# Loading the last head's output-projection rows once: 28 heads on 112 partitions, three heads in rows of 3 KB

## The chip, the cores and the metric

The kernel runs on one core of one Trainium2 chip. The time is the device time in microseconds (us) of one execution; a time given for a kernel is the median of several executions. Beside these, one execution was taken by the hardware profiler, which gives the start and length of every instruction and DMA packet. The engines are called PE (TensorE: matmuls, with its weight loads listed apart as PEld), DVE (VectorE), ACT (ScalarE), POOL (GpSimd) and SP (SyncE, which here issues nearly all DMA transfers). Memory on the chip has 128 partitions.

## The reference, cut to what matters

One token is decoded by an attention block and, beside it, by a SwiGLU block; a sigmoid gate mixes the two. All data are bf16.

```
x = A_x                                              # [1, 1, 512]
g = sigmoid((x * gate_w).sum(-1))
q = (x @ wq) as 32 heads of 128
p = softmax(q . k_cache^T * 128**-0.5)               # k_cache, v_cache: [1, 32, 65536, 128]
o = p @ v_cache                                      # 32 heads of 128, side by side: 4096 values
a = o @ wo                                           # wo: [4096, 512]
b = (silu(x @ w_gate) * (x @ w_up)) @ w_down         # w_gate, w_up: [512, 1792]; w_down: [1792, 512]
out = g * a + (1 - g) * b
```

The two caches hold 1074 MB of the 1088 MB that the kernel reads; every byte of a cache is used once.

## The kernel before, in words

**Tiling.** A head's K or V is two transfers of 8 MB (64 KB on each of 128 partitions, A and B half) into `ring`, a buffer of 176 KB per partition whose parts are used over and over. DVE turns the K rows in chunks into `kt` (four buffers, line 277), PE makes scores from a turned chunk (line 345) into `psS`; the softmax runs over POOL (195, 198), ACT (232) and DVE (301); PE then multiplies 256 + 256 weight tiles of V with the probabilities (line 352) into `psO`. DVE scales a head's output into `lt` (line 291), while the next head is already under way.

**Queues.** SP's program (lines 131 to 177) is an order written out by hand, with semaphore waits that hold a transfer until its place in `ring` is free. For each head it has: K's A half, the head before's V B half, K's B half, V's A half. All of it goes to one DMA queue, which works in order. A semaphore rises by 16 when a transfer has landed.

**The start.** The query projection weights `wq` are loaded first, then head 0's K in four pieces. PE projects the query (line 333), ACT copies it (216), PE spreads it with the constant `sel` (339), ACT copies it to `qd` and `zq` (220, 210), and then scores can begin. POOL builds `sel` and the identity `ident` in lines 181 to 190: two memsets and five affine selects, the last of which raises `s_sel`, on which PE waits in line 337.

**The output projection of heads 0 to 30.** It is done in the last head (number L = 31), in PE's block `pe_wo` (line 417), between the B half of head 30's V and the B half of head 31's scores. `wo` lies in the first 32 KB of `ring`, with 32 consecutive rows of `wo` on each partition: partitions 0 to 123 hold heads 0 to 30, and partitions 124 to 127 hold the rows of head 31, which meet zeros. It comes as two transfers of 16 KB on each of 128 partitions (lines 156 to 159), each after a wait for DVE to have turned the K that lay there. PE spreads the head outputs `lt` with `ident` to the same layout (line 420, into `psW`), ACT copies that to `om` (226), and PE multiplies column j of `om` with row j of every partition in `rows` (lines 358 and 359, half of the 512 outputs each). The last of these raises `s_wod`, after which SP issues the SwiGLU weights into the same place (164 to 166).

**The last head's rows.** Line 167 loads rows 3968 to 4095 of `wo`, 1 KB on each of 128 partitions, once more as `wo1`, since head 31's output comes at the very end. PE waits for them in line 431 (`s_wo1`), in its last block `pe_end`, and uses them in line 435 with `o31`, between the last two 128-row pieces of the down weights.

**The SwiGLU and the end.** PE's block `pe_mlp` (402 to 415) makes gate and up (line 408) and multiplies 12 of the 14 pieces of the down weights (414, after waits for `s_gu` and `s_wd`). After it PE multiplies the B half of head 31's V, which comes in six pieces (`PARTS`, line 113), the last ones small. Then come the last two down-weight pieces (`s_wd2`, `s_wd3`), two copies, and the output's transfer.

**Buffers at the start.** `xrow` and `gwrow` (1 KB per partition) and `xg` (2 KB) serve only the gate's sum at the start (lines 126, 212, 263, 324).

Of the kernel before, what the change touches and what calls it, by code (L numbers as in the profile page):

```python
# [5 lines left out]
P = 128  # L6
KB = 1024
# [8 lines left out]
ALU = mybir.AluOpType  # L16
ACT = mybir.ActivationFunctionType
ET = mybir.EngineType
BF16 = mybir.dt.bfloat16
F32 = mybir.dt.float32  # L20
# [6 lines left out]
def bass_gated_mix__mha_block_cached__swiglu_ffn__decode_kernel(  # L27
# [13 lines left out]
    _, H, S, Dh = A_k_cache.shape  # L41
    D = A_wq.shape[0]
# [5 lines left out]
    SCALE = float(Dh) ** -0.5  # L48
    assert Dh == 128 and D == 512 and F % P == 0 and ROWS == 256 and H == 32
    L = H - 1  # L50
    A_ORDER = list(range(NCH // 2, NCH)) + list(range(NCH // 2))
    B_ORDER = list(range(NCH))
    PER = 2 * NCH

    with ExitStack() as ctx:
        def sb(name, shape, dt):
            return ctx.enter_context(nc.sbuf_tensor(name, shape, dt))
# [12 lines left out]
        psW = psum("psW", [P, 512], F32)  # L70
# [8 lines left out]
        lt = sb("lt", [P, 4 * (P + 4) + 4], BF16)  # L79
        ident = sb("ident", [P, P], BF16)  # L80
        sel = sb("sel", [P, 4, 128], BF16)
        om = sb("om", [P, 32], BF16)
        o31 = sb("o31", [P, 2], BF16)
        ones1 = sb("ones1", [P, 2], BF16)
        onesr = sb("onesr", [P, P], F32)
        xrow = sb("xrow", [P, D], BF16)
        gwrow = sb("gwrow", [P, D], BF16)
        xg = sb("xg", [P, D], F32)
        fin = sb("fin", [P, D], BF16)
        sc = sb("sc", [P, 8], F32)  # L90
        xTb = sb("xTb", [P, 16], BF16)
# [17 lines left out]
        def at(byte, n):  # L109
            return ring[:, byte // 2:byte // 2 + n]  # L110
# [7 lines left out]
        wu_ap = at(WU, Dc * F).rearrange("p (c m j) -> p c m j", c=Dc, j=FC)  # L118
        wd_ap = at(WD, FC * D).rearrange("p (c n) -> p c n", c=FC)
        wo_ap = at(WO, 32 * D).rearrange("p (j n) -> p j n", j=32)  # L120
        wo1_ap = at(WO1, D)
        ktb = [kt[:, b, :].bitcast(BF16).rearrange("p (j n e) -> p j n e", j=2, e=2) for b in range(NB)]
        zw = [[zq[:, je, 31 - c:31 - c + P] for c in range(2 * NCH)] for je in range(4)]
# [7 lines left out]
        @block.sync  # L131
        def _(sp):
            def load(dst, src, s):
                sp.dma_start(dst, src).then_inc(sm[s], 16)  # L134

            def place(kind, h, u, s):
                byte = {"k": (K_A, K_B), "v": (V_A, V_B)}[kind][u]
                load(at(byte, ROWS * Dh), kv_dram[kind][h, u], s)

            k0 = kv_dram["k"][0, 0]  # L140
            k1 = kv_dram["k"][0, 1]
            half = ROWS * Dh // 2
            load(at(K_A + 2 * half, half), k0[:, half:2 * half], "s_ka")
            load(at(K_A, half), k0[:, 0:half], "s_k0a")
            load(at(K_B + 2 * half, half), k1[:, half:2 * half], "s_k0b")
            sp.wait_ge(sm["ktd"], NCH // 2)
            load(at(K_B, half), k1[:, 0:half], "s_kb")
            sp.wait_ge(sm["s_q"], 1)
            place("v", 0, 0, "s_va")
            for r in range(1, H):  # L150
                sp.wait_ge(sm["ktd"], PER * r - NCH // 2)
                place("k", r, 0, "s_ka")
                sp.wait_ge(sm["va1"], r)
                place("v", r - 1, 1, "s_vb")
                if r == L:
                    wo_dram = A_wo.rearrange("(p j) n -> p (j n)", j=32)
                    for q in range(2):
                        sp.wait_ge(sm["ktd"], PER * r + 3 * NCH // 4 + q * NCH // 4)
                        load(at(WO + q * 16 * KB, 16 * D), wo_dram[:, q * 16 * D:(q + 1) * 16 * D], "s_wo")
                sp.wait_ge(sm["ktd"], PER * r + NCH // 2)  # L160
                place("k", r, 1, "s_kb")
                sp.wait_ge(sm["vbd"], r + 1)
                place("v", r, 0, "s_va")
            sp.wait_ge(sm["s_wod"], 1)
            load(at(WG, Dc * F), B_w_gate.rearrange("(p c) f -> p (c f)", c=Dc), "s_wg")
            load(at(WU, Dc * F), B_w_up.rearrange("(p c) f -> p (c f)", c=Dc), "s_wu")
            load(at(WO1, D), A_wo[L * Dh:H * Dh, :], "s_wo1")
            sp.wait_ge(sm["ktd"], PER * H)
            wd_dram = B_w_down.rearrange("(p c) n -> p (c n)", c=FC)
            load(at(WD, WD_CUT * D), wd_dram[:, 0:WD_CUT * D], "s_wd")  # L170
            last = kv_dram["v"][L, 1]
            for n, ((r0, r1), s) in enumerate(zip(PARTS, MARKS)):
                if n == 1:
                    sp.wait_ge(sm["va1"], H)
                load(at(V_B + r0 * 256, (r1 - r0) * Dh), last[:, r0 * Dh:r1 * Dh], s)
            for j, s in ((FC - 2, "s_wd2"), (FC - 1, "s_wd3")):
                load(at(WD + 2 * j * D, D), wd_dram[:, j * D:(j + 1) * D], s)

        @block.gpsimd
        def _(pool):  # L180
            nc.gpsimd.memset(ident[:], 0.0)
            nc.gpsimd.memset(sel[:], 0.0).then_inc(sm["s_sel0"], 1)  # L182
            pool.wait_ge(sm["s_sel0"], 1)
            for je in range(4):
                off = 64 * (je // 2) + je % 2
                v = sel[:, je, :].rearrange("p (g d) -> p g d", g=4)
                last = nc.gpsimd.affine_select(out=v, in_=v, compare_op=ALU.not_equal, fill=1.0, base=-off,  # L187
                                               pattern=[[0, 4], [-2, 32]], channel_multiplier=1)
            nc.gpsimd.affine_select(out=ident[:], in_=ident[:], compare_op=ALU.not_equal, fill=1.0, base=0,  # L189
                                    pattern=[[-1, P]], channel_multiplier=1).then_inc(sm["s_sel"], 1)  # L190
            for m, n in enumerate(MARKS[1:]):
                nc.gpsimd.memset(hbuf[:, m], 0.0).then_inc(sm[n], 16 * L)  # L192
            for h in range(H):
                pool.wait_ge(sm["s_mx"], h + 1)
                nc.gpsimd.partition_all_reduce(amx, mxs, P, RMAX).then_inc(sm["s_ar"], 1)  # L195
                pool.wait_ge(sm["s_exp"], h + 2)
                pool.wait_ge(sm["s_li"], h + 1)  # L197
                nc.gpsimd.partition_all_reduce(Lt, rsum, P, RADD).then_inc(sm["s_L"], 1)  # L198

        @block.scalar  # L200
        def _(act):
# [21 lines left out]
            for h in range(H):  # L223
                if h == L:
                    act.wait_ge(sm["s_o"], 1)
                    nc.scalar.copy(om[:], psW[:, 0:32]).then_inc(sm["s_om"], 1)
                act.wait_ge(sm["s_ar"], h + 1)
                nc.scalar.mul(nbias, amx, -SCALE).then_inc(sm["s_nb"], 1)  # L228
                act.wait_ge(sm["s_nb"], h + 1)
                if h:  # L230
                    act.wait_ge(sm["s_pb"], h)
                nc.scalar.activation(pa[:], psS[:], ACT.Exp, bias=nbias, scale=SCALE,  # L232
                                     accum_out=rsum).then_inc(sm["s_exp"], 1)
                if h < L:
                    take_q(h + 1)
# [83 lines left out]
        def _(pe):  # L319
# [82 lines left out]
            with nc.body("pe_mlp", valid_engines=only):  # L402
                pe.wait_ge(sm["s_wg"], 16)
                pe.wait_ge(sm["s_wu"], 16)
                for j in range(FC):
                    for w, o in ((wg_ap, 64), (wu_ap, 80)):
                        for c in range(Dc):
                            last = nc.tensor.matmul(psM[:, o + j:o + j + 1], w[:, c, :, j], xTb[:, c:c + 1],  # L408
                                                    start=(c == 0), stop=(c == Dc - 1))
                last.then_inc(sm["s_h"], 1)  # L410
                pe.wait_ge(sm["s_gu"], 1)
                pe.wait_ge(sm["s_wd"], 16)
                for j in range(WD_CUT):
                    rows(guT[:, j:j + 1], wd_ap[:, j, :])
                nc.br("pe_vb", engines=only)

            with nc.body("pe_wo", valid_engines=only):
                pe.wait_ge(sm["s_otn"], H + 1)
                for q in range(4):
                    last = nc.tensor.matmul(psW[:, 0:32], lt[:, 4 + (P + 4) * q:4 + (P + 4) * q + P],  # L420
                                            ident[:, 32 * q:32 * q + 32], start=(q == 0), stop=(q == 3))
                last.then_inc(sm["s_o"], 1)
                pe.wait_ge(sm["s_om"], 1)
                pe.wait_ge(sm["s_wo"], 32)
                for j in range(32):
                    last = rows(om[:, j:j + 1], wo_ap[:, j, :], first=(j == 0))
                last[1].then_inc(sm["s_wod"], 1)
                nc.br("pe_kb", engines=only)

            nc.switch_bb("pe_end")  # L430
            pe.wait_ge(sm["s_wo1"], 16)
            pe.wait_ge(sm["s_wd2"], 16)
            rows(guT[:, FC - 2:FC - 1], wd_ap[:, FC - 2, :])
            pe.wait_ge(sm["s_o31"], 1)
# [36 lines left out]
```

## Time and profile before

| what | value |
|---|---|
| time, median of 3 runs (lowest to highest) | 2519.21 us (2519.11 to 2519.81) |
| the profiled execution's own time | 2519.56 us |
| its span, from the first to the last instruction | 2518.1 us |
| instructions | 45868 |
| read from HBM | 1087.77 MB, 432 GB/s over the span |
| busy: PE, PEld, DVE | 62%, 33%, 49% |
| busy: ACT, POOL | 2%, 1% |
| mean granted TensorE clock | 0.725 of full speed |

Times inside the trace are counted from the start of the span. A line of instructions has the start, the length, the engine, the kernel's line, the operation, what it writes and reads, and in brackets how long the engine had idled and what ended that. SPq is SP issuing a transfer: its length is that of issuing, not of the data's coming. In a line of waits the numbers are the total in us, how often, and the longest. A DMA packet is one contiguous piece that one of the core's 16 DMA engines moves, or the 4-byte write to a semaphore behind a transfer.

### The profile page before, as it was taken

Reading aid. Unit: us, or ns where it says so; the run is one execution under the profiler, and the core shown is the slowest. Engines: PE = TensorE matmul, PEld = TensorE weight load, DVE = VectorE, ACT = ScalarE, POOL = GpSimd, SP = SyncE. Lnnn points to the kernel's source line nnn. Section 1 sums busy time; section 2 is a strip of 40 time slices with the busy share of each in tenths; the row PEclk is TensorE's granted clock in tenths of the full one; section 3 lists DMA queues with packets and bytes.
Section 4 is the critical chain, followed back from the end, with each engine's and each line's share of the span. In section 5 each row is a group of like instructions: output and inputs, shape, how many; then the busy total and the mean of one; then the engine's idle time right before and its main releaser. Section 6 shows DMA issues by size and latency. Waiting matters only on the chain.

```text
span 2518.1 us, 45868 instructions
## 1 busy us (share of the span) xinstructions
PE 1561.7 (62%) x20700; PEld 837.3 (33%) x20828; DVE 1221.5 (49%) x1176; ACT 40.3 (2%) x138; POOL 26.1 (1%) x80
## 2 busy tenths in 40 slices
PE   4665755756657556566575575665755656656666
PEld 2333323323333233332332332333323333333234
DVE  4453553544535536445355354453553544545533
ACT  0000000000000000000000000000000000000000
POOL 0000000000000000000000000000000000000000
PEclk9776776767767677677677776776777767767776
DMA  9999999999999999999999999999999999999999
GB/s 417 435 435 433 433 435 434 433 433 433 433 433 433 433 433 433 433 433 433 433 433 433 433 433 434 434 433 435 436 433 433 433 434 433 433 433 433 434 432 393
DMA packets 20755, 1087.94 MB, mean 432 GB/s; under 512 B 2308, under 2 KB 2951, under 8 KB 3079
## 3 DMA queue, kind: packets, MB, share of 16 engines
q1 hardware_dynamic: 20736, 1087.78, 99.9%
q8 instruction: 8, 0.13, 0.0%
q14 instruction: 5, 0.03, 0.0%
q10 hardware_dynamic: 6, 0.00, 0.0%
HBM read 1087.77 MB, written 0.00 MB: 432 GB/s over the span
## 4 chain that ended last, share of the span: by engine, by line
issue 96%; ACT 1%; POOL 1%; DMA 1%; PE 0%; SPq 0%; DVE 0%; POOLq 0%
ACT pa L232 1%; DMA ring<-in_B_w_down_dram 1%; POOL st L198 0%; POOL st L195 0%; ACT st L228 0%; PE psO L352 0%; SPq L134 0%; POOL sel L187 0%; PE psY L358 0%; DVE pb L301 0%; POOLq L197 0%; POOL sel L182 0%; DVE fin L316 0%; POOL hbuf L192 0%; POOL ident L189 0%
## 5 line engine op out<-in xcount | busy, mean ns | idle before, releaser
L345 PE MATMUL psS<-kt,zq 128*128 128x512 bf16 x3968 | 1104.3, 424 | 827.9 <-DVE kt L277 805.4
L277 DVE STREAM_TRANSPOSE kt<-ring 128x1024 uint32<-128x1024 uint32 x1024 | 1163.2, 1206 | 925.2 <-DMA ring<-in_A_k_cache_dram 925.2
L345 PEld LDWEIGHTS psS<-kt,zq 128*128 128x128 bf16 x4096 | 387.4, 105 | 1518.1 <-DVE kt L277 1054.0
L352 PE MATMUL psO<-pb,ring 128*128 128x1 bf16 x16384 | 439.1, 164 | 109.7 <-DVE pb L301 102.5
L352 PEld LDWEIGHTS psO<-pb,ring 128*128 128x128 bf16 x16384 | 433.6, 101 | 140.7 <-issue 122.2
L291 DVE TENSOR_SCALAR lt<-psO,st,sc 128x4 f32 x32 | 9.4, 293 | 247.2 <-PE psO L352 247.2
L301 DVE STREAM_TRANSPOSE pb<-pa 128x512 bf16<-128x512 bf16 x32 | 22.8, 711 | 48.8 <-ACT pa L232 48.8
L228 ACT ACTIVATE st<-st 128x1 f32<-128x1 f32 x32 | 6.5, 203 | 2384.2 <-POOL st L195 2384.2
L299 DVE TENSOR_REDUCE st<-psS 128x1 f32<-128x512 f32 x32 | 22.1, 691 | 37.4 <-PE psS L345 37.4
L195 POOL PARTITION_ALL_REDUCE st<-st x32 | 11.3, 353 | 2410.1 <-DVE st L299 2410.1
L232 ACT ACTIVATE pa<-psS,st 128x512 bf16<-128x512 f32 x32 | 22.0, 687 | 1.0
L198 POOL PARTITION_ALL_REDUCE st<-st x32 | 12.3, 385 | 36.4 <-ACT pa L232 36.4
L210 ACT COPY zq<-qd 128x16 bf16<-128x16 bf16 x32 | 7.9, 248 | 0.0
L314 DVE TENSOR_TENSOR o<-psO,st 128x1 bf16<-128x1 f32 x1 | 0.2, 161 | 14.6 <-PE psO L352 14.6
L308 DVE TENSOR_SCALAR hbuf<-hbuf 128x14 f32<-128x14 f32 x1 | 0.2, 174 | 13.9 <-ACT hbuf L237 13.9
L408 PE MATMUL psM<-xTb,ring 128*128 128x1 bf16 x112 | 6.9, 198 | 0.0
L408 PEld LDWEIGHTS psM<-xTb,ring 128*128 128x128 bf16 x112 | 6.8, 163 | 0.0
L358 PE MATMUL psY<-ring,om 128*1 128x256 bf16 x32 | 4.9, 327 | 2.3 <-DMA ring<-in_A_wo_dram 2.3
L333 PE MATMUL psM<-xTb,ring 128*128 128x1 bf16 x128 | 3.6, 165 | 4.3 <-DMA ring<-in_A_wq_dram 4.3
L232 ACT ACTIVATION_READ_ACCUMULATOR pa<-psS,st 128x1 f32 x32 | 6.2, 193 | 0.0
L324 PE MATMUL psM<-ones,xrow 1*128 1x1 bf16 x4 | 0.3, 172 | 7.9 <-DMA gwrow<-in_gate_w_dram 7.9
L333 PEld LDWEIGHTS psM<-xTb,ring 128*128 128x128 bf16 x128 | 3.5, 104 | 4.4 <-issue 4.4
(57 smaller groups left out, 39.4 us busy)
## 6 DMA issues: line engine op xcount, KB each, us to landing
ring<-in_A_k_cache_dram SPq DMA_DIRECT2D x4, 4096.0 KB, 27.4
ring<-in_A_wq_dram SPq DMA_DIRECT2D x1, 4096.0 KB, 12.6
ring<-in_A_wo_dram SPq DMA_DIRECT2D x2, 2048.0 KB, 10.6
ring<-in_A_v_cache_dram SPq DMA_DIRECT2D x1, 3776.0 KB, 18.1
ring<-in_A_v_cache_dram SPq DMA_DIRECT2D x1, 2048.0 KB, 18.3
ring<-in_B_w_gate_dram SPq DMA_DIRECT2D x1, 1792.0 KB, 37.9
ring<-in_B_w_up_dram SPq DMA_DIRECT2D x1, 1792.0 KB, 41.9
ring<-in_B_w_down_dram SPq DMA_DIRECT2D x1, 1536.0 KB, 13.8
```

The source lines that it names most:

```text
L195: nc.gpsimd.partition_all_reduce(amx, mxs, P, RMAX).then_inc(sm["s_ar"], 1)
L198: nc.gpsimd.partition_all_reduce(Lt, rsum, P, RADD).then_inc(sm["s_L"], 1)
L210: nc.scalar.copy(zq[:, :, 31:128:32], qd[:, h]).then_inc(sm["s_zq"], 1)
L232: nc.scalar.activation(pa[:], psS[:], ACT.Exp, bias=nbias, scale=SCALE, accum_out=rsum).then_inc(sm["s_exp"], 1)
L277: nc.vector.transpose(o, src).then_inc(sm["ktd"], 1)
L291: nc.vector.tensor_scalar(lt[:, bass.ds(i * 4, 4, P + 5)], psO[:, 0:1].to_broadcast([P, 4]), Li, sc[:, 3:4], ALU.mult, ALU.mult).then_inc( ...
L299: nc.vector.reduce_max(mxs, psS[:], AX_X).then_inc(sm["s_mx"], 1)
L301: nc.vector.transpose(pb[:], pa[:]).then_inc(sm["s_pb"], 1)
L333: last = nc.tensor.matmul(psM[:, 128 + h:129 + h], wq_ap[:, c, h * Dh:(h + 1) * Dh], xTb[:, c:c + 1], start=(c == 0), stop=(c == Dc - 1))
L345: last = nc.tensor.matmul(psS[:], zw[je][c], ktb[n % NB][:, je // 2, :, je % 2], start=first and je == 0, stop=stop and je == 3)
L352: last = nc.tensor.matmul(psO[:, 0:1], at(base + r * 256, Dh), pb[:, col:col + 1], start=first and n == 0, stop=stop and n == len(rows) - 1)
L408: last = nc.tensor.matmul(psM[:, o + j:o + j + 1], w[:, c, :, j], xTb[:, c:c + 1], start=(c == 0), stop=(c == Dc - 1))
```

## The change

Heads 0 to 27 of `wo` (3584 rows) are laid out as before, 32 rows to a partition, but on 112 partitions, still in two transfers of 16 KB per partition. Heads 28 to 30 (384 rows) come in a third transfer, three rows (3 KB) to each of 128 partitions, into a new buffer `xwo` that takes in the former `xrow`, `gwrow` and `xg`. Head 31's rows are loaded by line 167 alone. For the new layout POOL builds a constant `spread` (1152 elements per partition: one memset, one affine select) before `sel`'s affine selects; PE has nine matmuls of one column more ahead of ACT's copy (35 columns instead of 32), multiplies on 112 partitions, and has three further pairs of row products. PE's wait for `s_wo1` stands in `pe_mlp`, ahead of that for `s_wd`, instead of in `pe_end`.

```diff
+    WP = 112
+    HX = WP // 4
+    NX = L - HX
...
+        spread = sb("spread", [P, NX, NX, P], BF16)
+        om = sb("om", [P, 32 + NX], BF16)
...
-        xrow = sb("xrow", [P, D], BF16)
-        gwrow = sb("gwrow", [P, D], BF16)
-        xg = sb("xg", [P, D], F32)
+        xwo = sb("xwo", [P, 4 * D], BF16)
+        xrow, gwrow, xg = xwo[:, 0:D], xwo[:, D:2 * D], xwo[:, 2 * D:4 * D].bitcast(F32)
+        wox = xwo[:, 0:NX * D]
...
+        wox_ap = wox.rearrange("p (j n) -> p j n", j=NX)
...
-                    wo_dram = A_wo.rearrange("(p j) n -> p (j n)", j=32)
+                    wo_dram = A_wo[0:32 * WP, :].rearrange("(p j) n -> p (j n)", j=32)
                     for q in range(2):
                         sp.wait_ge(sm["ktd"], PER * r + 3 * NCH // 4 + q * NCH // 4)
-                        load(at(WO + q * 16 * KB, 16 * D), wo_dram[:, q * 16 * D:(q + 1) * 16 * D], "s_wo")
+                        load(at(WO + q * 16 * KB, 16 * D)[0:WP, :], wo_dram[:, q * 16 * D:(q + 1) * 16 * D], "s_wo")
+                    load(wox, A_wo[32 * WP:L * Dh, :].rearrange("(p j) n -> p (j n)", j=NX), "s_wo")
...
             nc.gpsimd.memset(ident[:], 0.0)
+            nc.gpsimd.memset(spread[:], 0.0)
             nc.gpsimd.memset(sel[:], 0.0).then_inc(sm["s_sel0"], 1)
             pool.wait_ge(sm["s_sel0"], 1)
+            nc.gpsimd.affine_select(out=spread[:], in_=spread[:], compare_op=ALU.not_equal, fill=1.0, base=0,
+                                    pattern=[[P, NX], [-1, NX], [-NX, P]], channel_multiplier=1)
...
-                    nc.scalar.copy(om[:], psW[:, 0:32]).then_inc(sm["s_om"], 1)
+                    nc.scalar.copy(om[:], psW[:, 0:32 + NX]).then_inc(sm["s_om"], 1)
...
                 pe.wait_ge(sm["s_gu"], 1)
+                pe.wait_ge(sm["s_wo1"], 16)
                 pe.wait_ge(sm["s_wd"], 16)
...
                 for q in range(4):
-                    last = nc.tensor.matmul(psW[:, 0:32], lt[:, 4 + (P + 4) * q:4 + (P + 4) * q + P],
-                                            ident[:, 32 * q:32 * q + 32], start=(q == 0), stop=(q == 3))
+                    nc.tensor.matmul(psW[:, 0:32], lt[:, 4 + (P + 4) * q:4 + (P + 4) * q + P],
+                                     ident[:, 32 * q:32 * q + 32], start=(q == 0), stop=(q == 3))
+                for j in range(NX):
+                    for x in range(NX):
+                        c = 4 + 4 * (HX + x)
+                        last = nc.tensor.matmul(psW[:, 32 + j:33 + j], spread[:, x, j, :], lt[:, c:c + 1],
+                                                start=(x == 0), stop=(x == NX - 1))
                 last.then_inc(sm["s_o"], 1)
                 pe.wait_ge(sm["s_om"], 1)
-                pe.wait_ge(sm["s_wo"], 32)
+                pe.wait_ge(sm["s_wo"], 48)
                 for j in range(32):
-                    last = rows(om[:, j:j + 1], wo_ap[:, j, :], first=(j == 0))
+                    rows(om[0:WP, j:j + 1], wo_ap[0:WP, j, :], first=(j == 0))
+                for j in range(NX):
+                    last = rows(om[:, 32 + j:33 + j], wox_ap[:, j, :])
                 last[1].then_inc(sm["s_wod"], 1)
                 nc.br("pe_kb", engines=only)
 
             nc.switch_bb("pe_end")
-            pe.wait_ge(sm["s_wo1"], 16)
             pe.wait_ge(sm["s_wd2"], 16)
```

More of the change, by code (lines that the diff above doesn't have):

```diff
@@ L81, in bass_gated_mix__mha_block_cached__swiglu_ffn__decode_kernel @@
         sel = sb("sel", [P, 4, 128], BF16)
-        om = sb("om", [P, 32], BF16)
+        spread = sb("spread", [P, NX, NX, P], BF16)
+        om = sb("om", [P, 32 + NX], BF16)
         o31 = sb("o31", [P, 2], BF16)
```

## The prediction, made before the changed kernel ran

> **What bounds the kernel now.** I read the page first: its rows by slices, then the DMA queues.
>
> ```profile
> span 2518.1 us, 45868 instructions
> ...
> DMA  9999999999999999999999999999999999999999
> GB/s 417 435 435 433 433 435 434 433 433 433 433 433 433 433 433 433 433 433 433 433 433 433 433 433 434 434 433 435 436 433 433 433 434 433 433 433 433 434 432 393
> ...
> q1 hardware_dynamic: 20736, 1087.78, 99.9%
> ```
>
> SP's queue (q1) holds the 16 DMA engines for 99.9% of the span, at 433 GB/s in nearly every slice, while PE is busy 62% and DVE 49%. The packets confirm it: the queue's first starts at 1.73 us, its last ends at 2515.47 us, and in any 0.5 us between, hardly an exception, 16 of 16 engines have one in hand. So the time is 1.7 us of start, what each engine must move, and a tail; anything else counts only if it lets that queue run dry.
>
> The chain of waits shows the tail (start, length, what):
>
> ```profile
> 2493.62 21.95 DMA ring<-in_B_w_down_dram
> 2515.57 0.14 issue
> 2515.70 0.37 PE psY L358
> ...
> 2516.54 0.41 DVE fin L316
> ```
>
> The last packets are the down weights' last kilobytes; 2.5 us after they land the span ends. Then the two stages that the change touches, in order of time. First the start:
>
> ```profile
> 0.72 0.21 POOL L181 MEMSET ident<- 128x128 bf16 x1 [0.29 <-POOLq L456]
> ...
> 0.86 0.53 POOL L182 MEMSET sel<- 128x512 bf16 x1
> ...
> 13.94 1.10 POOL L187 TENSOR_SCALAR_AFFINE_SELECT sel<-sel 128x128 bf16<-128x128 bf16 x4 [12.54 <-issue]
> 15.00 0.28 POOL L189 TENSOR_SCALAR_AFFINE_SELECT ident<-ident 128x128 bf16<-128x128 bf16 x1
> ...
> 17.32 0.19 PEld L339 LDWEIGHTS psQ<-qTb,sel 128*128 128x128 bf16 x4 [0.36 <-ACT qTb L216]
> ...
> 19.52 0.26 ACT L210 COPY zq<-qd 128x16 bf16<-128x16 bf16 x1
> 24.05 1.25 DVE L277 STREAM_TRANSPOSE kt<-ring 128x1024 uint32<-128x1024 uint32 x1 [14.10 <-DMA ring<-in_A_k_cache_dram]
> ```
>
> POOL's constants are ready at 15.28 us; PE takes them at 17.32; the query is ready at 19.78; scores begin when the first K chunk is turned, at 25.3 us. And the last head:
>
> ```profile
> 2428.93 4.83 SPq L134 DMA_DIRECT2D ring<-in_A_wo_dram  x2
> ...
> 2433.81 0.43 SPq L134 DMA_DIRECT2D ring<-in_A_k_cache_dram  x1
> ...
> 2441.82 0.29 PE L420 MATMUL psW<-ident,lt 128*128 128x32 bf16 x4 [0.50 <-DVE lt L291]
> 2442.14 0.19 ACT L226 CAST om<-psW 128x32 bf16<-128x32 f32 x1 [44.02 <-PE psW L420]
> ...
> 2444.36 0.37 PE L358 MATMUL psY<-ring,om 128*1 128x256 bf16 x1 [2.25 <-DMA ring<-in_A_wo_dram]
> ...
> 2449.31 0.33 SPq L134 DMA_DIRECT2D ring<-in_B_w_gate_dram  x1
> ...
> 2463.69 18.15 DVE L277 STREAM_TRANSPOSE kt<-ring 128x1024 uint32<-128x1024 uint32 x16 [21.92 <-DMA ring<-in_A_k_cache_dram]
> ```
>
> PE has `om` at 2442.33 and waits 2 us for `wo`; its row products end at 2449.27; then PE and DVE idle until K's B half lands at 2463.69.
>
> **The bytes.** The change loads 3968 + 128 rows of 1 KB instead of 4096 + 128: 131072 bytes less, 0.30 us at 433 GB/s. By packets: those of 16 KB took 615 ns (median), of 1792 bytes 74 ns, of 4608 bytes 180 ns, of 1 KB 46 ns, of 64 KB 2422 ns, a semaphore write 9 ns. Between the rows of 1792 and 4608 bytes, one of 3072 takes 74 + 1280/2816 x 106 = 122 ns. Before, each engine moves 2 x 8 packets of 16 KB, 9.84 us. After, if 112 rows share out evenly, 2 x 7 packets (8.61), 8 of 3 KB (0.98) and one semaphore write more (0.01): 9.60 us. That is **-0.24 us**, all on the path, since all engines are full.
>
> How 112 rows share out, no row shows. The queue's 20736 packets are 144 transfers (the sum of the issues on the page) x (128 + 16): 128 rows always go to 16 engines. The three one-row transfers (x, the gate weights, the output) make six packets, one engine each. So the number of engines follows the shape. I bound it: 16 engines with 7 rows each, -0.24 us; 14 engines with 8 rows each, where those 14 keep their 9.84 us and get 0.99 more, +0.99 us; eight engines with 14 rows, 28 x 0.615 + 0.99 - 9.84 = +8.4 us; and one, 224 x 0.615 + 0.99 - 9.84 = +129 us. I take the first: 112 is 16 x 7, and 128, its nearest row, is shared out evenly.
>
> [...]
>
> The third load's memory side is one contiguous block of 128 x 3 KB, the same kind as `wq` (128 x 32 KB), which landed in 12.6 us with 16 engines at work; so it costs as reckoned.
>
> **SP.** One more issue, 0.43 us by the row of its neighbour at 2433.81. Behind it stands K's B half, issued at 2434.3 then. The queue holds both `wo` transfers until 2444.2; 9.9 us of cover, no cost. If the cover were gone it would cost those 0.43 us.
>
> **POOL at the start.** The memset: 0.53 us for 512 elements and 0.21 for 128 give 0.83 ns each, 1.06 us for 1152. The affine select: 0.275 us for 128 elements, nine times that is 2.5 us; between 0.28 (if the time were all fixed) and, as a doubling for its pattern of three dimensions, 5.0. I take 2.5; 3.5 us in all, 6.1 at most. Whether the 12.54 us wait moves with the memset I can't tell; I let it. `s_sel` then comes at 18.8 instead of 15.28, 1.5 us too late for PE; the query is ready at 21.3, still 4 us before the first turned chunk. Cover in all: 2.05 + 5.5 = 7.6 us. No cost. The other way round, constants that come later can't gain anything.
>
> **PE in the last head.** Nine matmuls of one column with their weight loads: 0.25 us at the 28 ns of the query projection (128 in 3.55 us), 1.5 us at that row's single length of 165 ns. `om` comes at 2443.9 at worst; `wo`, all of it, lands some 0.24 us earlier than 2444.3, so cover is left: 0.2 us, thin, and then 14 us before K's B half lands. Three further pairs of products: 0.11 us (2448.67 to 2448.78) to 0.21 us a pair, 0.6 at most. `s_wod` and SP's gate-weight issue come by about 0.4 us later than 2449.31; behind that issue stand the up weights and `wo1`, but the queue holds V's A half until 2482.9 (41.6 us after its issue at 2441.35). No cost. Rows of products on 112 partitions instead of 128: same columns, same time.
>
> **The moved wait.** `wo1` lands 41.8 us after its issue at 2450.16, at 2492.0, and PE reaches the down-weight block at 2501.06, after `guT`. Cover 9.1 us: nothing waits. Behind it would stand 12 down-weight pieces and the 192 V tiles. In `pe_end` the wait goes from ahead of one that ends later anyway; at most the 0.14 us between landing and first matmul, and I take nothing, since the last two kilobytes of down weights still have to land.
>
> **Code.** Some 30 more PE instructions and one more transfer in SP's program. Instruction fetches come as 16 KB packets of their own queue (eight, 0.94 to 1.07 us each); the 64 KB packet beside the one at 2446 us took 3.02 instead of 2.42 us. One more fetch would cost one engine up to 0.6 us. Since engines end 0.5 us apart (last starts 2514.88 to 2515.42), that is +0.1 to +0.6 us at the end; I take no further fetch.
>
> **Sum.** -0.24 us. The profiled execution took 2519.56 us, 1.46 beyond its span, and would take 2519.3; it stands 0.35 above the median of the runs, from which the forecast is 2519.21 - 0.24 = **2519.0 us**. A difference under 0.2% (5 us) is about what can't be told from no change here.
>
> **Rivals.** *A fetch, or a shifted tail, eats the gain*: up to +0.6 - 0.24, 2519.6 us. For it: fetches do fall into this stage (2446 us). Against: the added code is some 30 instructions beside some 1280 matmuls and weight loads of PE's loop, which with the rest took only eight fetches.
> *14 engines*: 2520.2 us. For it: 8 rows per engine is what every transfer here has. Against: nothing forces it when 7 fit.
> *Few engines, slower*: eight engines give 2527.6 us, one 2648; it passes the 5 us mark when the fullest engine gets more than 23 of the 224 row packets, 11 or 12 rows a transfer. For it: one-row transfers use a single engine. Against: 112 has factors of 16 and 14.
> *POOL lets the queue run dry at the start*: needs more than 7.6 us on POOL before scores are late, and then SP's next K piece (issued after 33 us) is late against a queue that is full until 40 us (16.8 MB issued by then at 433 GB/s). Only some 13 us begin to cost and 18 cost 5 us. Against: 6.1 us at most.
>
> **Chances.** As reckoned, 80%; gain eaten, 9%; 14 engines, 7%; few engines 2%; POOL 1%; something unseen on the fast side 1%. Range of the first alone: 2518.6 to 2519.4, as the runs before spread. The whole range reaches to 14 engines: 2518.5 to 2520.3. Slower by over 0.2% are few engines and POOL, 3%; faster 1%; within, 96%.
>
> **What would show it.** SP's queue with 20736 - 32 + 144 = 20848 packets and 1087.65 MB (20844 packets if 14 engines); `zq` copied by 22 us and the first transpose still at about 24 us; PE's wait for `wo` still ended by the DMA; the gate weights issued near 2449.7; no wait on `wo1`; the same 2.5 us tail. Wrong it would be if the DMA row showed a slice under 9, or the last packets of the engines ended over 1 us apart.

## The result, and the profile after

The changed kernel takes 2528.66 us (median of 7 runs, 2527.01 to 2530.29), the kernel before, measured beside it, 2519.69 us (7 runs, 2519.08 to 2519.95). The ratio is 1.0036, 95% interval 1.0026 to 1.0045: slower by 9 us, where 2519.0 us was forecast, in a range up to 2520.3.

The page of the changed kernel, first its span, the rows by slices and the DMA queues:

```profile
span 2527.6 us, 46029 instructions
...
DMA  9999999999999999999999999999999999999999
GB/s 422 432 431 434 432 437 434 431 436 434 431 432 433 437 434 432 434 435 432 432 431 437 435 432 432 435 432 432 432 437 435 432 432 434 434 431 434 437 366 390
...
q1 hardware_dynamic: 20848, 1087.64, 99.9%
...
HBM read 1087.64 MB, written 0.00 MB: 430 GB/s over the span
```

The bytes are those forecast to 0.01 MB (1087.64 against 1087.65), and so are the packets, 20848: the loads of `wo` ran on 16 engines. In the records of packets one packet of an engine starts where its last one ends, so the engines' chains can be followed: in most of them stand 7 packets of 16 KB, a semaphore write, 7 more and another write. The DMA row shows no gap either. But the last slice but one, which holds the loads of `wo`, moved 366 GB/s instead of 432. A DMA engine that is busy need not be moving at its speed: the share of busy time hides this here, and the GB/s shows it.

The same six microseconds of both kernels, in the middle of the `wo` loads. The columns are the stretch, its length, busy time of PE, PEld, DVE, ACT and POOL, the granted clock, the DMA engines' busy share, GB/s. First before, then after:

```profile
2432.00:2438.00 6.00, 5.90 (x147) 4.14 (x146) 1.41 (x2) 0.00 (x0) 0.00 (x0) 0.89 0.93 396
```

```profile
2432.00:2438.00 6.00, 3.74 (x66) 2.04 (x66) 1.29 (x2) 0.00 (x0) 0.00 (x0) 1.00 0.89 208
```

About the same busy share, half the bytes. The DMA issues of the changed kernel say which transfers it is (KB each, median us from issue to landing):

```profile
ring<-in_A_wo_dram SPq DMA_DIRECT2D x2, 1792.0 KB, 16.9
...
xwo<-in_A_wo_dram SPq DMA_DIRECT2D x1, 384.0 KB, 20.2
```

Before, the two larger transfers took 10.6 us:

```profile
ring<-in_A_wo_dram SPq DMA_DIRECT2D x2, 2048.0 KB, 10.6
```

In the trace's records of packets, the 224 packets of 16 KB on 112 partitions took 1157 ns on the mean (659 to 1692), where the 256 on 128 partitions had taken 615 (611 to 625).

The end of the timeline is the old one, some 9.5 us later, with the copy of the output starting 0.9 us after the last landing at 2525.16:

```profile
2525.20 0.37 PE L367 MATMUL psY<-ring,guT 128*1 128x256 bf16 x1
...
2526.04 0.41 DVE L325 CAST fin<-psY 1x256 bf16<-1x256 f32 x1 [0.73 <-PE psY L367]
...
2526.48 0.23 ACTq L250 DMA_DIRECT2D out_dram<-fin  x1
```

**Where the 9.5 us of the profiled executions (2529.07 against 2519.56) are**, per engine, from the packets:

| packets | before | after | difference, us per engine |
|---|---|---|---|
| `wo`, 16 KB | 16 of 615 ns | 14 of 1157 ns | 16.20 - 9.84 = +6.36 |
| third load, 3 KB | none | 8 of 216 ns, reckoned 122 | +1.73 |
| 64 KB packets of V and K just ahead of and behind the `wo` loads | 2422 ns | 26 of them slower, up to 4036 ns, 19.5 us in all | 19.5 / 16 = +1.22 |
| sum | | | +9.31 |

For the rest, 0.2 us, no row was found.

### The profile page after: what moved, and what is told of

Same layout as the page of the kernel before. It is cut to its first block, busy times and chain, and to the rows that moved or that the text cites. A ratio compares the mean times of both kernels' runs of the same rounds, so it can differ in the third digit from the quotient of the medians.

```text
span 2527.6 us, 46029 instructions
## 1 busy us (share of the span) xinstructions
PE 1593.4 (63%) x20843; PEld 838.6 (33%) x20843; DVE 1221.6 (48%) x1176; ACT 40.3 (2%) x138; POOL 28.3 (1%) x82
## 3 DMA queue, kind: packets, MB, share of 16 engines
q1 hardware_dynamic: 20848, 1087.64, 99.9%
HBM read 1087.64 MB, written 0.00 MB: 430 GB/s over the span
## 4 chain that ended last, share of the span: by engine, by line
issue 96%; ACT 1%; POOL 1%; DMA 1%; PE 0%; SPq 0%; DVE 0%; POOLq 0%
ACT pa L241 1%; DMA ring<-in_B_w_down_dram 1%; POOL st L207 0%; POOL st L204 0%; ACT st L237 0%; PE psO L361 0%; SPq L139 0%; POOL spread L191 0%; POOL sel L196 0%; POOL spread L188 0%; PE psY L367 0%; DVE pb L310 0%; POOLq L206 0%; POOL sel L189 0%; DVE fin L325 0%
## 5 line engine op out<-in xcount | busy, mean ns | idle before, releaser
L354 PE MATMUL psS<-kt,zq 128*128 128x512 bf16 x4096 | 1134.2, 426 | 796.7 <-DVE kt L286 778.6
L367 PE MATMUL psY<-ring,om 112*1 112x256 bf16 x32 | 6.2, 384 | 9.6 <-DMA xwo<-in_A_wo_dram 9.6
L368 PE MATMUL psZ<-ring,om 112*1 112x256 bf16 x32 | 6.2, 386 | 0.0
## 6 DMA issues: line engine op xcount, KB each, us to landing
ring<-in_A_wo_dram SPq DMA_DIRECT2D x2, 1792.0 KB, 16.9
```

The costliest lines, as they stand in the source:

```text
L354: last = nc.tensor.matmul(psS[:], zw[je][c], ktb[n % NB][:, je // 2, :, je % 2], start=first and je == 0, stop=stop and je == 3)
L367: a = nc.tensor.matmul(psY[0:1, 0:half], lhs, rhs[:, 0:half], start=first, stop=stop)
```

## The experiments

Each is compared with the kernel before in the same series of runs.

**Is it the transfers over 112 partitions, or the rest of the change?** Two kernels split the change. The first keeps all of it but gives the two big loads 128 partitions again:

```diff
-                    wo_dram = A_wo[0:32 * WP, :].rearrange("(p j) n -> p (j n)", j=32)
+                    wo_dram = A_wo.rearrange("(p j) n -> p (j n)", j=32)
...
-                        load(at(WO + q * 16 * KB, 16 * D)[0:WP, :], wo_dram[:, q * 16 * D:(q + 1) * 16 * D], "s_wo")
+                        load(at(WO + q * 16 * KB, 16 * D), wo_dram[:, q * 16 * D:(q + 1) * 16 * D], "s_wo")
```

> The changed kernel, with its two big wo loads on all 128 partitions again (as before: 32 rows each, head 31's rows among them, unused); the third load of 3 KB rows, spread, the 35 columns and the moved wait stay. Theory 1 (the transfers over 112 partitions are slow in themselves: in the changed kernel's trace their 16 KB packets take 1157 ns on the mean, 615 before): back to packets of 615 ns, 3 KB packets at the reckoned 122 ns, so 2519.7 + 0.98 = 2520.7 us. Theory 2 (the cost lies in the rest: the third load, its wait, PE's and POOL's new work, the longer code): it stays near 2528.7 us.

Measured: 2520.12 us against 2519.58, ratio 1.0003 (0.9993 to 1.0012). The 16 KB packets took 615 ns again, the 3 KB packets 122.6, just as reckoned; the last packet ended at 2516.41 us in the trace against 2515.47 before, the +0.94 that those eight packets cost. So beyond these packets the third load, its wait, `spread`, PE's nine matmuls and the moved wait cost nothing that shows, and the loss goes with the 112 partitions.

The second does that one part alone, in the kernel before:

```diff
-                        load(at(WO + q * 16 * KB, 16 * D), wo_dram[:, q * 16 * D:(q + 1) * 16 * D], "s_wo")
+                        load(at(WO + q * 16 * KB, 16 * D)[0:112, :], wo_dram[0:112, q * 16 * D:(q + 1) * 16 * D], "s_wo")
```

> The kernel before, with nothing changed but that its two wo loads take 112 partitions instead of 128 (the rows of heads 28 to 31 are not loaded, so what PE multiplies with there is old data: the output leaves out three heads). Theory 1: 14 packets of some 1157 ns per engine instead of 16 of 615, +6.4 us, and up to 1 us more from neighbouring packets: 2526 to 2527 us. Theory 2: 14 x 0.615 instead of 16 x 0.615, 2518.5 us.

Measured: 2527.56 us against 2519.58, ratio 1.0033 (1.0020 to 1.0045); 16 KB packets of 1168 ns. One slice of partitions in one line makes nearly the whole loss.

```profile
2432.00:2438.00 6.00, 4.04 (x87) 2.61 (x86) 0.85 (x1) 0.00 (x0) 0.00 (x0) 0.82 0.89 208
```

The same 208 GB/s in the same six microseconds as in the changed kernel. Theory 2 is out.

**The side of HBM, or the side of the buffer?** The changed kernel with its reads made contiguous, the partitions kept:

```diff
-                    wo_dram = A_wo[0:32 * WP, :].rearrange("(p j) n -> p (j n)", j=32)
+                    wo_dram = A_wo[0:32 * WP, :].rearrange("(q p j) n -> q p (j n)", q=2, j=16)
...
-                        load(at(WO + q * 16 * KB, 16 * D)[0:WP, :], wo_dram[:, q * 16 * D:(q + 1) * 16 * D], "s_wo")
+                        load(at(WO + q * 16 * KB, 16 * D)[0:WP, :], wo_dram[q], "s_wo")
```

> The changed kernel, with the same bytes on the same 112 partitions, but each transfer reads one contiguous block of 1.75 MB (16 KB per partition without a gap) where the changed kernel reads 16 KB out of every 32 KB (the rows of wo then meet the wrong heads: the output is not the attention's). Theory 1a (the cost lies on the side of the chip's buffer, in which partitions the engines write at a time): no change, 2527 to 2530 us with 16 KB packets of 1.0 to 1.2 us. Theory 1b (it lies in how the engines' addresses in HBM stand to each other): the packets change, towards 615 ns and 2519.5 us.

Measured: 2528.62 us, ratio 1.0036 (1.0023 to 1.0048), packets of 1167 ns. Nothing changed: theory 1a.

And the same 3584 rows on all 128 partitions:

```diff
-                    wo_dram = A_wo[0:32 * WP, :].rearrange("(p j) n -> p (j n)", j=32)
+                    wo_dram = A_wo[0:32 * WP, :].rearrange("(p j) n -> p (j n)", j=28)
...
-                        load(at(WO + q * 16 * KB, 16 * D)[0:WP, :], wo_dram[:, q * 16 * D:(q + 1) * 16 * D], "s_wo")
+                        load(at(WO + q * 14 * KB, 14 * D), wo_dram[:, q * 14 * D:(q + 1) * 14 * D], "s_wo")
```

> The changed kernel, with the same 3584 rows of wo laid on all 128 partitions, 28 rows each, two transfers of 14 KB per partition (PE's products read the buffer as in the changed kernel, so the output is not the attention's). Theory 1a: 16 packets of 540 ns (the row of the gate weights' 14336 bytes) and 8 of 122 ns instead of 16 of 615, 9.63 instead of 9.84: 2519.5 us, the forecast's gain of 0.2 us or so. Theory 1b leaves this open, since the addresses differ too. Theory 2: 2528.7 us.

Measured: 2518.82 us against 2519.58, ratio 0.9998 (0.9988 to 1.0007). The packets of 14 KB took 540 ns, those of 3 KB 122; the last packet ended at 2515.29 us, 0.18 earlier than before. That is about the gain that was forecast (0.21 by this layout's packets), from the same bytes, but it is read from one profiled execution of each kernel; the ratio's interval takes in no change, and the medians' 0.76 us can't be told from none.

```profile
ring<-in_A_wo_dram SPq DMA_DIRECT2D x2, 1792.0 KB, 9.2
...
xwo<-in_A_wo_dram SPq DMA_DIRECT2D x1, 384.0 KB, 10.2
```

The same 1792 KB as in the changed kernel land 9.2 us after their issue instead of 16.9.

**Which partitions?** All of these are the kernel before with its two loads cut to some partitions; the diff is that of the second kernel above with other bounds: `[0:64]`, `[32:96]`, `[0:96]` and `[16:128]`, on the buffer's and on `wo`'s side alike.

> The kernel before, with its two wo loads cut to partitions 0 to 63 (heads 16 to 31 of wo are not loaded; PE multiplies old data there, so the output is not the attention's). 64 rows are 4 per engine. [...] Theory R (only the number of rows decides, an uneven or small number per engine being slow): the same time as the run on partitions 32 to 95. Without any slowing: 8 x 0.615 instead of 16 x 0.615, 2514.7 us. [...]

Measured: 2522.65 us against 2519.27, ratio 1.0013 (1.0004 to 1.0023). The 16 KB packets took 1318 ns on the mean, 2.1 times the 615 on all 128 partitions, and 64 KB packets around them took 2.3 us per engine more: half the bytes of `wo`, and slower than all of them on 128 partitions.

> The same as the run on partitions 0 to 63, but on partitions 32 to 95 (heads 8 to 23 of wo loaded, the others not). [...] Theory R: the same time as on partitions 0 to 63.

Measured: 2515.23 us, ratio 0.9984 (0.9974 to 0.9993); packets of 674 ns on the mean, 611 in the median. Theory R falls: the number of rows is the same, and the two runs are 7.4 us apart. The two kernels' rows of issues, partitions 0 to 63 first:

```profile
ring<-in_A_wo_dram SPq DMA_DIRECT2D x2, 1024.0 KB, 14.1
```

```profile
ring<-in_A_wo_dram SPq DMA_DIRECT2D x2, 1024.0 KB, 6.9
```

> The kernel before, with its two wo loads cut to partitions 0 to 95 (heads 24 to 31 of wo not loaded). [...] Theory R has no number for it; without any slowing 12 x 0.615, 2517.1 us.

Measured: 2525.97 us, ratio 1.0026 (1.0016 to 1.0036), packets of 1173 ns: 8.9 us above the time without any slowing. Twelve packets (6 rows per engine, two transfers) of 1173 ns instead of 615 make 6.7 us of that per engine, and 64 KB packets around the loads took 2.1 us per engine longer.

> The kernel before, with its two wo loads on partitions 16 to 127 (heads 0 to 3 of wo not loaded): again 112 rows, 7 per engine, but with the full half above. [...] If only the start or the end of the range decided (partition 112 to 127 left empty), it would be another time, towards 2518.5 us.

Measured: 2528.16 us, ratio 1.0036 (1.0023 to 1.0049), packets of 1190 ns: much as on partitions 0 to 111 (2527.56 us, 1168 ns), and not towards 2518.5 us.

**Two partitions further on, and a control.** The first has partitions 34 to 97 (bounds `[34:98]` on both sides), again 64 rows, two partitions on from 32 to 95. The second has partitions 32 to 95, read from the addresses that the slow run on 0 to 63 had used:

```diff
-                        load(at(WO + q * 16 * KB, 16 * D), wo_dram[:, q * 16 * D:(q + 1) * 16 * D], "s_wo")
+                        load(at(WO + q * 16 * KB, 16 * D)[32:96, :], wo_dram[0:64, q * 16 * D:(q + 1) * 16 * D], "s_wo")
```

> The kernel before, with its two wo loads cut to partitions 34 to 97 (64 rows, the other rows of wo not loaded; the output is not the attention's). [...]

Measured: 2519.12 us against 2519.57, ratio 0.9999 (0.9989 to 1.0008), which lies between the other two runs of 64 rows: 3.9 us more than on partitions 32 to 95 (2515.23), 3.5 less than on 0 to 63 (2522.65), with packets of 1049 ns on the mean (10 of 128 under 700). Two partitions' difference in the place takes away nearly all that half the bytes had saved.

> The kernel before, with its two wo loads cut to partitions 32 to 95 as in the fast run of 64 rows, but read from the addresses of the slow one (the rows that partitions 0 to 63 have in wo; the output is not the attention's). Theory P (the place in the chip's buffer decides): 2515.2 us as there. If the place in HBM decided: 2522.7 us as on partitions 0 to 63.

Measured: 2515.20 us, ratio 0.9983 (0.9974 to 0.9993), packets of 632 ns, 611 in the median. Between these runs the addresses in HBM make no difference; the place in the buffer does. The six microseconds of these two kernels, partitions 34 to 97 first:

```profile
2432.00:2438.00 6.00, 4.74 (x95) 2.83 (x94) 1.50 (x2) 0.00 (x0) 0.00 (x0) 0.90 0.92 232
```

```profile
2432.00:2438.00 6.00, 5.95 (x165) 4.46 (x165) 0.96 (x1) 0.00 (x0) 0.00 (x0) 0.97 1.14 478
```

A share above 1, and 478 GB/s where the other slices hold 433, show that the counting is not exact in so short a stretch. So the packets' own lengths decide: at 1049 ns against 632 the loads on 34 to 97 move 0.6 as much.

## Why the prediction was wrong

**The step that failed** is in "The bytes": "After, if 112 rows share out evenly, 2 x 7 packets (8.61)". The rows do share out evenly, over 16 engines, as the prediction took it: 20848 packets, and not the 20844 of 14 engines, and 7 packets to a chain. What failed is the price of a packet. The 615 ns were measured where 128 rows go to all partitions, and were carried over to 112 as if a packet's time hung on its length alone. It measured 1157 ns: 16.2 us per engine instead of 8.6. The prediction bounded how many engines would work, and not how fast each would; no range of its kind could have held this. Nor did either of its signs of being wrong appear: the DMA row has no slice under 9, and the last sixteen packets of 1 KB start within 0.7 us (2524.36 to 2525.00).

The other terms of the sum:

- The third load: 8 x 0.122 us was right where the engines were in step (122.6 ns with 128 partitions ahead of it). In the changed kernel it measured 216 ns, behind and beside the slow packets.
- What wasn't in the sum at all: 26 of the 64 KB packets just ahead of and behind the slow loads took longer too, 1.2 us per engine.
- The price of a further instruction fetch was misread: the packet of 3.02 us lies at 57.6 us, and the 64 KB packet just behind the fetch at 2446 us took 2.92. No further fetch came (eight, as before), so nothing hung on it.
- POOL at the start: the memset of `spread` took 1.06 us, as reckoned. The affine select took 1.22 us, half of the 2.5 taken and between the ends. The long wait ahead of it didn't move with the memset (it ended at 13.70 us). The query was ready at 20.2 us and the first transpose began at 23.89: covered, as forecast.

```profile
0.86 1.06 POOL L188 MEMSET spread<- 128x1152 bf16 x1
...
13.70 1.22 POOL L191 TENSOR_SCALAR_AFFINE_SELECT spread<-spread 128x1152 bf16<-128x1152 bf16 x1 [11.31 <-issue]
...
19.91 0.26 ACT L219 COPY zq<-qd 128x16 bf16<-128x16 bf16 x1
23.89 1.25 DVE L286 STREAM_TRANSPOSE kt<-ring 128x1024 uint32<-128x1024 uint32 x1 [13.89 <-DMA ring<-in_A_k_cache_dram]
```

- PE in the last head: the nine matmuls took 0.38 us, near the lower bound. The row products on 112 partitions went at the pace of those on 128, a pair every 0.21 us at first and every 0.11 later. PE waited 9.6 us for `wo` instead of 2.2, and the gate weights were issued at 2460.57 instead of 2449.31. That cost nothing by itself, as forecast: V's A half kept the queue full until 2492.5 (49.1 us after its issue at 2443.44). The loss is in the DMA engines' time, not in a queue run dry.

```profile
2444.04 0.38 PE L435 MATMUL psW<-lt,spread 128*128 128x1 bf16 x9
...
2453.98 0.37 PE L367 MATMUL psY<-ring,om 112*1 112x256 bf16 x1 [9.56 <-DMA xwo<-in_A_wo_dram]
...
2460.57 0.33 SPq L139 DMA_DIRECT2D ring<-in_B_w_gate_dram  x1
...
2473.32 18.14 DVE L286 STREAM_TRANSPOSE kt<-ring 128x1024 uint32<-128x1024 uint32 x16 [29.46 <-DMA ring<-in_A_k_cache_dram]
```

- The moved wait: `wo1` landed at 2501.5 us (40.1 after its issue at 2461.42), and PE reached the down-weight block at 2510.7. Nothing waited.
- The rival of few engines gave 2527.6 us, close to the measured time, but that is chance: its mechanism would show in the number of packets, and does not.

## What to carry to other kernels

The time of a DMA packet here hung on which partitions its load filled, and not only on its own length: 16 KB took 615 ns on 0 to 127, 674 on 32 to 95 and 1318 on 0 to 63. Before a transfer is cut to fewer partitions, time one of that very shape, and lay the same bytes on all 128 partitions instead if that can be done: here 1792 KB landed 9.2 us after their issue instead of 16.9. Where DMA bounds a kernel, read the GB/s of a stage beside its busy share: here 208 and 396 GB/s stood beside shares of 0.89 and 0.93. A price from a row is a price for that row's shape: here a saving of 0.24 us, worked out to the nanosecond, stood against an unasked question worth 9 us.

## What the runs showed of the hardware

Unexpected was how the speed of a load hangs on the partitions that it fills. All loads below are two transfers of 16 KB per partition on 16 engines, with 64 KB packets ahead of and behind them (in the changed kernel and its variant with contiguous reads the 3 KB load stands between):

| partitions | rows per engine | mean 16 KB packet, ns | us per engine |
|---|---|---|---|
| 0 to 127 | 8 | 615 | 9.84 |
| 32 to 95 | 4 | 674, 632 | 5.39, 5.06 |
| 34 to 97 | 4 | 1049 | 8.39 |
| 0 to 63 | 4 | 1318 | 10.54 |
| 0 to 95 | 6 | 1173 | 14.08 |
| 0 to 111 | 7 | 1157, 1168, 1167 | 16.20, 16.36, 16.34 |
| 16 to 127 | 7 | 1190 | 16.65 |

That the place in the buffer decides is shown for 64 rows, by 32 to 95 against 0 to 63 and by the control with exchanged addresses. For 112 rows the contiguous reads speak against the side of HBM and 16 to 127 comes out like 0 to 111; but every run of 112 rows was slow, so that the place, and not the 7 rows per engine, makes them slow is argued from the 64 rows.

What makes some of these loads slow is not shown. 64 rows took 674, 1049 and 1318 ns a packet on 32 to 95, 34 to 97 and 0 to 63, all on 16 engines, and the records of packets don't say which partition a packet goes to, nor in which order an engine goes through its rows. In the six microseconds above the changed kernel moved 208 GB/s, 0.48 of the 433 that nearly every slice of the kernel before shows. Nearly all its packets came out near twice the time (206 of the 224 between 900 and 1500 ns, one under 700), rather than some at 615 ns and some much slower; why stays open too.

Also open is what a full kernel with the 28-row layout would gain: it would need another way to spread the heads' outputs, which wasn't tried, for at most some 0.2 us, while the runs of the kernel before lie 0.9 to 1.4 us apart within one series.
